# The first chunk's attention logits as one group of eighty matmuls, with the mask added by VectorE and the task order searched anew

## The chip, the cores and the metric

One core of a Trainium2 chip. The metric is the device time of one execution in microseconds; medians are given over several executions. Single core, so there is one span and one granted clock per run; an execution over 1.5% above the fastest of its kernel was classed as slow and left out of the ratios.

Short names: TensorE does the matmuls, VectorE the elementwise work on bf16 and the softmax sums, ScalarE the gelu, the exp and most copies out of PSUM ("evictions"), GpSimd the accumulating output writes, SyncE issues transfers. ScalarE also issues some transfers from its own instruction stream.

## The reference, cut to what matters

```python
def reference(A_x, A_wqkv, A_wo, B_x, B_w1, B_b1, B_w2, B_b2):   # x is 1 x 2048 x 640, bf16
    xn = _layernorm(x, axis=-1)
    return x + _A_ref(xn, A_wqkv, A_wo) + _B_ref(xn, B_w1, B_b1, B_w2, B_b2)
# _A_ref: 32 heads of 20; position s attends to s, s-2, s-4, ... s-14 (8 offsets, "w")
    mask = idx >= 0                                  # only the first 14 positions lose anything
    logits = jnp.einsum("bhsd,bhswd->bhsw", q, kg) * scale
    logits = jnp.where(mask[None, None, :, :], logits, -1e9)
    attn = _softmax(logits, axis=-1)
    o = jnp.einsum("bhsw,bhswd->bhsd", attn, vg)     # then @ wo
# _B_ref: gelu(xn @ w1 + b1) @ w2 + b2, with 1536 hidden units
```

The kernel handles the 2048 positions in four chunks of 512 ("chunk 0" to "chunk 3"). The mask concerns chunk 0 alone.

## The kernel before

It isn't written as loops. A small planner holds tasks with an engine, a guessed duration, a rank and their needs, runs them through a model of the engines, and emits them in the order in which the model started them. Each engine then executes its own list strictly in that order. A table of rank offsets, found by search, decides the order.

```python
RANK = {
    "ad02": 35.3, "av1": -101.7, "av2": 76.7, ...      # cut: 22 entries
}
...
        for wp in range(W // 2):                     # a pair of offsets; wp = 0..3
            ...                                      # qk{n}{wp}{i}: VectorE, q * shifted k -> "prod"
            if wp % 2:
                both = [("prod", "qk", n, wp - 1), pr]
                need = [...]
                pl.add(f"lg{n}{wp}", PE, 1.2, n - 1000, need, f("lg", n, wp), both + [L], slack=0.8)
        ...
        pl.add(f"m{n}", VE, 1.22, n - 1000, [f"lg{n}3"], f("max", n), [L, m])
        ...                                          # mx (subtract), ex (exp), ss (sum), ri (reciprocal), at (attn)
        pl.add(f"xs{n}", SE, 1.2, n - 1000, [f"at{n}"], f("xs", n), [at, ax])
        pl.add(f"xd{n}", DQ, 6.0, n - 1000, [f"at{n}"], f("xd", n), [at, ax])
        ...                                          # av: VectorE, v * broadcast attn -> "pv"; ad, ot: their sums -> oT
```

Logits are per-head sums of products, so TensorE makes them with a 0/1 matrix of heads: forty matmuls for four offsets. In chunk 0 each such group of forty ended in one more matmul, a row of ones times a row of mask values, which accumulates -1e9 into the masked places.

```python
    def do_lg(n, wp):
        L = get(("L", n), lambda: psL.tile([P, W, P], F32, tag="L", name="L"))
        for x in range(2):
            prod = tiles["qk", n, wp - 1 + x]
            logits(L, prod, wp - 1 + x)
        if n == 0:
            g = slice(2 * wp - 2, 2 * wp + 2)
            nc.tensor.matmul(L[0:H, g, 0:MW], lhsT=ones_r[:], rhs=maskrow[:, g, :],
                             start=False, stop=False, skip_group_check=True)
```

After the softmax the weights are broadcast over partitions by four transfers: two issued by SyncE, two by ScalarE.

The stream of matmuls uses four rotating PSUM banks (`psA`, tag "acc") for projections (`pps`) and the first MLP layer (`hps`). ScalarE empties them; when it is late, TensorE stands.

Task names: `pj` a projection group of five matmuls, `pc` its eviction, `pad` the copy of the last 14 columns of K or V into the next chunk's buffer, `lg` logits, `mk` the new mask instruction, `xb` the addition of the MLP's bias to x on VectorE, `xs` and `xd` the two halves of a broadcast, `av` the products with V. The first digit is the chunk.

Of the kernel before, what the change touches and what calls it, by code (L numbers as in the profile page):

```python
# [11 lines left out]
ALU = mybir.AluOpType  # L12
AX = mybir.AxisListType
BF16 = mybir.dt.bfloat16
F32 = mybir.dt.float32
PE, VE, SE, DQ = "pe", "ve", "se", "dq"


class Plan:
# [101 lines left out]
S, D, F, H, W, DIL = 2048, 640, 1536, 32, 8, 2  # L121
# [10 lines left out]
MASKED = -1e9  # L132
MW = 16
# [5 lines left out]


RANK = {
    "ad02": 35.3, "av1": -101.7, "av2": 76.7, "f10": 53.1, "f11": 23.2, "f12": 66, "f13": 190, "gj1": -337.3,
    "gj3": -98.6, "o01": -72.1, "o03": 12.1, "o22": 213.2, "pj11": -45.8, "pj30": 109.2, "pj32": 49.6, "qk1": 10.4,
    "qk2": 112.3, "rc1": -399, "st2": 79.8, "xb1": -67.6, "xb3": 55.5, "xn1": 47.4,
}


def make_plan(fns, offsets=RANK):

    pl = Plan(offsets)  # L150
# [6 lines left out]
    def f(kind, *a):  # L157
        return lambda: fns[kind](*a)

    def done(n, which):  # L160
        if n:
            return [f"pc{n}{which}{to}" for to in range(KT)]
        return [f"gc{bl}{g}" for bl in range(BPC) for g, parts in enumerate(GROUPS) if which in [p[0] for p in parts]]

    for n in range(NCH):
# [36 lines left out]
        for which, buf in enumerate((q, k, v)):  # L202
# [5 lines left out]
            if which:  # L208
                need = done(n - 1, which) if n else []
# [3 lines left out]
        L = ("L", n)  # L213
        for wp in range(W // 2):
            pr = ("prod", "qk", n, wp)
            for i in range(2):
                need = done(n, 0) + done(n, 1) + [f"pad{n}1"]
                pl.add(f"qk{n}{wp}{i}", VE, 1.42, base + 3.0 * wp + i, need, f("qk", n, wp, i), [q, k, pr])
            if wp % 2:
                both = [("prod", "qk", n, wp - 1), pr]  # L220
                need = [f"qk{n}{x}{i}" for x in (wp - 1, wp) for i in range(2)] + ([f"lg{n}{wp-2}"] if wp > 2 else [])
                pl.add(f"lg{n}{wp}", PE, 1.2, n - 1000, need, f("lg", n, wp), both + [L], slack=0.8)

        e, at, ax = ("e", n), ("attn", n), ("ax", n)
        m, rs, ss, z = ("m", n), ("rs", n), ("ss", n), ("prod", "z", n)
        pl.add(f"m{n}", VE, 1.22, n - 1000, [f"lg{n}3"], f("max", n), [L, m])
        pl.add(f"mx{n}", VE, 1.22, n - 1000, [f"m{n}"], f("sub", n), [L, m, z])
        pl.add(f"ex{n}", SE, 1.02, n - 1000, [f"mx{n}"], f("exp", n), [z, e], table="exp")
        pl.add(f"ss{n}", VE, 1.93, n - 1000, [f"ex{n}"], f("sum", n), [e, ss])
# [6 lines left out]
        for wp in range(W // 2):  # L236
            for i in range(2):
                need = [f"xd{n}", f"xs{n}", f"pad{n}2"] + done(n, 2)
                pl.add(f"av{n}{wp}{i}", VE, 1.42, base + 15.0 + 6.0 * wp + i, need, f("av", n, wp, i), [v, ax, prs[wp]])
        for k2, (a, b, r) in enumerate(((0, 1, 9.0), (2, 3, 21.0), (0, 2, 22.0))):  # L240
            need = [f"av{n}{x}{i}" for x in (a, b) for i in range(2)] if k2 < 2 else [f"ad{n}0", f"ad{n}1"]
# [8 lines left out]
        for bl in range(BPC):  # L250
# [4 lines left out]
            for pc in range(5):  # L255
                need = [last] if last else [f"ge{n}{ft}" for ft in range(FT)] + [f"xb{n}", "ld"]
# [15 lines left out]
def kernel(  # L272
# [16 lines left out]
    nc = tc.nc  # L289
# [6 lines left out]
    consts = ctx.enter_context(tc.tile_pool(name="consts", bufs=1))  # L296
# [46 lines left out]
    nc.gpsimd.memset(eps_t[:], EPS)  # L343
    warm = consts.tile([P, 1], F32, name="warm")
    nc.scalar.activation(warm[:], eps_t[:], ACT.Sqrt)
    ones_r = consts.tile([1, H], BF16, name="ones_r")
    nc.gpsimd.memset(ones_r[:], 1.0)
    maskrow = consts.tile([1, W, MW], BF16, name="maskrow")
    nc.gpsimd.memset(maskrow[:], 0.0)
    for w in range(1, W):  # L350
        nc.gpsimd.memset(maskrow[:, w, 0 : DIL * w], MASKED)
    head_of = consts.tile([P, H], BF16, name="head_of")
    b1T = consts.tile([P, FT], F32, name="b1T")

# [17 lines left out]
    tiles = {}  # L372

    def get(key, make):
        if key not in tiles:
            tiles[key] = make()
        return tiles[key]
# [139 lines left out]
            op=ALU.mult,  # L517
        )

    def do_lg(n, wp):  # L520
        L = get(("L", n), lambda: psL.tile([P, W, P], F32, tag="L", name="L"))
        for x in range(2):
            prod = tiles["qk", n, wp - 1 + x]
            logits(L, prod, wp - 1 + x)
        if n == 0:
            g = slice(2 * wp - 2, 2 * wp + 2)
            nc.tensor.matmul(
                L[0:H, g, 0:MW],
                lhsT=ones_r[:],
                rhs=maskrow[:, g, :],  # L530
                start=False,
                stop=False,
                skip_group_check=True,
            )

    def logits(L, prod, wp):
        for t in range(KT):
            for j in range(BPC):
                nc.tensor.matmul(
                    L[j * H : (j + 1) * H, 2 * wp : 2 * wp + 2, :],  # L540
                    lhsT=head_of[:],
                    rhs=prod[:, :, t, j * P : (j + 1) * P],
                    start=(t == 0 and wp % 2 == 0),
                    stop=(t == KT - 1 and wp % 2 == 1),
                    skip_group_check=True,
                )
# [155 lines left out]
    with tc.manual_schedule(engines=engines):  # L702

        idle = psA.tile([P, CH], F32, tag="acc", name="idle")
        for _ in range(WARM):
            nc.tensor.matmul(idle[:, 0:P], lhsT=ident[:], rhs=ident[:], start=True, stop=True)
        for t in make_plan(fns).run():
            t["fn"]()
# [30 lines left out]
```

## Time and profile before

| | |
|---|---|
| median, lowest, highest of the first 3 executions | 217.23, 216.60, 220.82 us |
| profiled span | 215.8 us |
| TensorE, VectorE, ScalarE busy | 208.0, 180.8, 107.2 us |
| TensorE idle, as drawn, 26 to 212 us | 0.7 us in three waits |
| chain of waits that ended last | TensorE 48%, VectorE 28%, transfers 16% |

Here is the stretch of that chain, for the kernel before (start, us, what):

```profile
52.90 1.57 SPq L596
54.52 6.85 DMA ax<-attn
...
82.71 1.49 DVE oT L627
84.20 1.40 DVE prod L513
...
97.70 0.59 ACTq L596
98.33 6.25 DMA ax<-attn
104.70 2.89 DVE pv L612 x2
...
115.46 7.02 DVE pv L612 x5
122.50 0.59 ACTq L596
123.13 1.68 ACTq L596
124.86 0.59 ACT vT L498
125.49 1.24 PE pps L463 x5
```

Read it from the bottom. It leads from a group of TensorE's matmuls at 125.49 through ScalarE's eviction of V, two transfer issues on ScalarE's own stream (ACTq) and VectorE back to the landing of the first broadcast at 61.4. The chain also crosses the second broadcast, 98.33 to 104.58, but over the same stretch VectorE works on five products of its own, to 104.68, and waits for that broadcast only 0.02 us.

### The profile page before, as it was taken

To read this page: it belongs to the slowest core of one execution; us is meant where nothing else is said; L and a number is where in the kernel's file an instruction comes from. 1 tells how busy PE (TensorE), PEld (TensorE's weight loads), DVE (VectorE), ACT (ScalarE), POOL (GpSimd) and SP (SyncE) were. 2 spreads that over 40 slices of the span, in tenths; PEclk is the share of its full clock that TensorE was granted. 3 is DMA by queue.
4 is the path that set the end of the run, shared out by engine and by line. 5 is a ranking of instruction groups with operands and counts; after the bars stand their busy time and mean duration, and the time that the engine had idled before them with its cause. 6 is when DMAs were issued, how large, how long until landed. Compare 5 with 4: busy or idle time off the path is not lost.

```text
span 215.8 us, 3941 instructions
## 1 busy us (share of the span) xinstructions
PE 208.0 (96%) x1669; PEld 121.6 (56%) x1692; DVE 180.8 (84%) x170; ACT 107.2 (50%) x190; POOL 14.5 (7%) x33
## 2 busy tenths in 40 slices
PE   7799999999999999999999999999999999999994
PEld 7699945555454545555555545566545455555552
DVE  3649899769989999999999999998999999982001
ACT  3466895796937476553276075213763521351210
POOL 2000000000000000101011000111100011101220
PEclk9999999999999999999999999999999999999999
DMA  6999316926981313507220370222111522215223
GB/s 219 364 365 355 76 30 160 390 74 153 254 82 30 61 30 33 152 0 156 74 30 0 38 186 3 30 33 27 20 18 19 176 30 27 20 17 122 33 30 62
DMA packets 21449, 21.49 MB, mean 100 GB/s; under 512 B 9016, under 2 KB 18616, under 8 KB 21432
## 3 DMA queue, kind: packets, MB, share of 16 engines
q1 hardware_dynamic: 17832, 16.49, 27.2%
q0 software_dynamic: 2160, 2.46, 9.6%
q10 hardware_dynamic: 1440, 2.29, 3.8%
q8 instruction: 13, 0.21, 0.4%
q14 instruction: 4, 0.03, 0.1%
HBM read 10.00 MB, written 5.08 MB: 70 GB/s over the span
## 4 chain that ended last, share of the span: by engine, by line
PE 48%; DVE 28%; DMA 16%; SPq 3%; issue 2%; ACTq 1%; ACT 1%; DVEq 0%
PE lo L665 18%; PE hps L634 14%; DVE pv L612 10%; PE gps L480 6%; DMA ax<-attn 6%; PE hi L667 6%; DMA wv_sb<-in_A_wqkv_dram 5%; DMA b2bc<-in_B_b_dram 5%; DVE pv L621 4%; DVE prod L513 3%; PE pps L463 3%; DVE ssum L574 3%; DVE x_sb L440 2%; DVE attn L586 2%; DVE rs L581 1%
## 5 line engine op out<-in xcount | busy, mean ns | idle before, releaser
L634 PE MATMUL hps<-xnT,w_sb 128*128 128x512 bf16 x236 | 54.2, 379 | 0.2
L665 PE MATMUL lo<-w_sb,hT 128*128 128x512 bf16 x183 | 51.9, 379 | 0.0
L612 DVE TENSOR_TENSOR pv<-vT,ax 128x2560 bf16<-128x2560 bf16 x32 | 45.8, 1485 | 0.6 <-DMA ax<-attn 0.5
L513 DVE TENSOR_TENSOR prod<-qT,kT 128x2560 bf16<-128x2560 bf16 x32 | 45.5, 1483 | 0.1
L667 PE MATMUL hi<-w_sb,hT 128*128 128x128 bf16 x192 | 40.3, 219 | 0.5
L645 ACT ACTIVATE hT<-hps,b1T 128x512 bf16<-128x512 f32 x48 | 31.7, 687 | 16.5 <-PE hps L634 14.6
L634 PEld LDWEIGHTS <-w_sb 128*128 128x128 bf16 x240 | 22.9, 98 | 26.5
L621 DVE TENSOR_TENSOR pv<-pv 128x5120 bf16<-128x5120 bf16 x12 | 33.8, 2824 | 0.3
L665 PEld LDWEIGHTS <-hT 128*128 128x128 bf16 x192 | 18.7, 98 | 22.7 <-issue 0.6
L672 ACT CAST osb<-lo 128x512 bf16<-128x512 f32 x15 | 8.8, 584 | 42.7 <-issue 22.8
L678 POOL DMA_DIRECT2D out_dram<-osb x15 | 13.1, 873 | 195.1 <-ACT osb L673 195.1
L665 PE MATMUL lo<-wo,oT 128*128 128x512 bf16 x77 | 22.6, 379 | 0.0
L667 PEld LDWEIGHTS <-hT 128*128 128x128 bf16 x192 | 18.4, 98 | 1.5
L463 PE MATMUL pps<-xnT,wv_sb 128*128 128x512 bf16 x72 | 17.2, 379 | 0.4 <-ACT vT L498 0.3
L667 PE MATMUL hi<-wo,oT 128*128 128x128 bf16 x80 | 16.9, 219 | 0.3 <-issue 0.2
L463 PE MATMUL pps<-xnT,wk_sb 128*128 128x512 bf16 x71 | 16.9, 380 | 0.3
L463 PE MATMUL pps<-xnT,wq_sb 128*128 128x512 bf16 x75 | 16.8, 379 | 0.2 <-ACT qT L498 0.2
L383 DVE BATCH_NORM_STATS2 stats<-x_sb 128x6 f32<-128x320 bf16 x16 | 7.4, 460 | 8.4 <-DMA x_sb<-in_A_x_dram 8.4
L686 DVE TENSOR_TENSOR osb<-lo,x_sb 128x512 bf16<-128x512 f32 x1 | 0.7, 692 | 16.1 <-PE lo L665 16.1
L498 ACT CAST vT<-pps 128x512 bf16<-128x512 f32 x15 | 8.2, 596 | 11.3 <-PE pps L463 11.3
L665 PEld LDWEIGHTS <-oT 128*128 128x128 bf16 x80 | 7.8, 98 | 9.9 <-DVE oT L627 0.6
L463 PEld LDWEIGHTS <-wq_sb 128*128 128x128 bf16 x75 | 8.8, 117 | 7.8 <-issue 0.5
(63 smaller groups left out, 213.1 us busy)
## 6 DMA issues: line engine op xcount, KB each, us to landing
w_sb<-in_B_w_dram SPq DMA_DIRECT2D x2, 1920.0 KB, 10.8
out_dram<-osb POOLq DMA_DIRECT2D x15, 160.0 KB, 3.4
ax<-attn ACTq DMA_DIRECT2D x8, 256.0 KB, 5.7
ax<-attn SPq DMA_DIRECT2D x8, 256.0 KB, 5.3
x_sb<-in_A_x_dram SPq DMA_DIRECT2D x3, 640.0 KB, 10.9
out_dram<-x_sb SPq DMA_DIRECT2D x3, 640.0 KB, 3.5
wq_sb<-in_A_wqkv_dram SPq DMA_DIRECT2D x1, 800.0 KB, 5.0
wk_sb<-in_A_wqkv_dram SPq DMA_DIRECT2D x1, 800.0 KB, 8.6
```

Of the source, the lines that this page charges most:

```text
L463: nc.tensor.matmul(ps[:], lhsT=wqkv_p[which][:, ti, to, :], rhs=xnT[:, ti, :], start=(ti == 0), stop=(ti == KT - 1),)
L480: nc.tensor.matmul(ps[:, i, :], lhsT=wqkv_p[which][:, ti, to, :], rhs=tiles["xnT", 0][:, ti, cs], start=(ti == 0), stop=(ti == KT - 1),)
L498: nc.scalar.copy(dest[:, to, off : off + CH], tiles["pps", n, which, to][:])
L513: nc.vector.tensor_tensor(out=prod[:, i, :, :], in0=qkv_tile(n, 0)[:], in1=qkv_tile(n, 1)[:, :, off : off + CH], op=ALU.mult,)
L612: nc.vector.tensor_tensor(out=pv[:, i, :, :].rearrange("p t (j c) -> p t j c", j=BPC), in0=qkv_tile(n, 2)[:, :, off : off + CH].rearrange( ...
L621: nc.vector.tensor_tensor(out=ta[:], in0=ta[:], in1=tb[:], op=ALU.add)
L634: nc.tensor.matmul(ps[:], lhsT=w1_sb[:, ti, ft * P : (ft + 1) * P], rhs=tiles["xnT", n][:, ti, :], start=(ti == 0), stop=(ti == KT - 1),)
L645: nc.scalar.activation(hT[:], tiles["hps", n, ft][:], ACT.Gelu_apprx_tanh, bias=b1T[:, ft : ft + 1], scale=1.0)
L665: nc.tensor.matmul(lo[:], lhsT=lhs, rhs=rhs[:, 0:CH], start=first, stop=last)
L667: nc.tensor.matmul(hi[:, 0 : D - CH], lhsT=lhs, rhs=rhs[:, CH:D], start=first, stop=last)
L672: nc.scalar.copy(osb[:, 0:CH], tiles["lo", n, bl][:])
L678: nc.gpsimd.dma_start(rows, tiles["osb", n, bl][:], accum_op=ALU.add)
```

## The change

Intent: two mask matmuls and one entry into a group of logit matmuls less for TensorE, in exchange for one small VectorE instruction. The rank table was searched anew for it, so the order of tasks changes on all engines as well.

```diff
 RANK = {
-    "ad02": 35.3, "av1": -101.7, "av2": 76.7, ... "xb1": -67.6, "xb3": 55.5, "xn1": 47.4,
+    "ad02": 77, "av2": -4.2, ... "rc3": -86.1, "st2": 49.8, "st3": 51.7, "xn2": 23.8,
 }                                                      # cut: 22 entries each
-            if wp % 2:
-                both = [("prod", "qk", n, wp - 1), pr]
-                ...
-                pl.add(f"lg{n}{wp}", PE, 1.2, n - 1000, need, f("lg", n, wp), both + [L], slack=0.8)
+            group = 2 if n else 4
+            if wp % group == group - 1:
+                wps = range(wp - group + 1, wp + 1)
+                ...
+                pl.add(f"lg{n}{wp}", PE, 0.16 + 0.52 * group, n - 1000, need, f("lg", n, wps), every + [L], slack=0.8)
...
+        if n == 0:
+            pl.add("mk", VE, 0.26, n - 1000, ["lg03"], f("mask"), [L])
...
-    maskrow = consts.tile([1, W, MW], BF16, name="maskrow")
+    mask = consts.tile([H, W, MW], F32, name="mask")
...
+    def do_mask():
+        L = tiles["L", 0]
+        nc.vector.tensor_tensor(out=L[0:H, :, 0:MW], in0=L[0:H, :, 0:MW], in1=mask[:], op=ALU.add)
```

## The prediction

> **What bounds the kernel now.** I read the page's busy line first, then its forty slices, the waits of TensorE, a table of busy time by stretch, and last TensorE and VectorE in order of time around the first chunk's logits.
>
> ```profile
> PE 208.0 (96%) x1669; PEld 121.6 (56%) x1692; DVE 180.8 (84%) x170; ACT 107.2 (50%) x190; POOL 14.5 (7%) x33
> ...
> PE   7799999999999999999999999999999999999994
> ...
> DVE  3649899769989999999999999998999999982001
> ```
>
> TensorE is busy in every slice from the third to the last but one; VectorE nearly so, but it has only its two last evictions left after the thirty-seventh. A busy TensorE row is no proof, so I asked what it waits for between 26 and 212 us:
>
> ```profile
> PE pps L463 <- ACT vT L498: 0.3, 1, 0.3
> PE pps L463 <- ACT qT L498: 0.2, 1, 0.2
> PE hi L667 <- issue: 0.2, 1, 0.2
> ```
>
> Three waits, 0.7 us in 186. The stretches say the same (after the stretch: its length, then busy us and count of PE, PEld, DVE, ACT, POOL, then clock, DMA share, GB/s):
>
> ```profile
> 26.50:60.00 33.50, 33.29 (x233) 17.33 (x239) 30.01 (x33) 26.74 (x43) 0.00 (x0) 1.00 0.62 174
> 60.00:110.00 50.00, 49.27 (x395) 27.05 (x393) 49.16 (x34) 24.18 (x41) 2.09 (x3) 1.00 0.34 65
> 110.00:160.00 50.00, 49.42 (x357) 26.71 (x361) 49.03 (x32) 24.73 (x41) 4.97 (x6) 1.00 0.25 41
> ```
>
> So the time is the start until all of wqkv is there (13.1 us), then one dense stream of matmuls to 212.8, then some 3 us of tail. The chain of waits goes through VectorE between 45 and 124 us; this doesn't make VectorE the bound, because TensorE leaves no gap there: two engines run side by side, both nearly full, and whichever is late at a meeting point stops the other. Only what shortens the TensorE stream, or makes it wait, moves the end. The part that changes, in order of time (start, us, engine, line):
>
> ```profile
> 26.50 6.64 PE L634 MATMUL hps<-xnT,w_sb 128*128 128x512 bf16 x29
> 33.07 1.28 PE L539 MATMUL L<-prod,head_of 128*32 128x256 bf16 x40
> 34.27 0.20 PE L527 MATMUL L<-maskrow,ones_r 1*32 1x64 bf16 x1
> 34.41 2.33 PE L634 MATMUL hps<-xnT,w_sb 128*128 128x512 bf16 x9
> 36.58 2.32 PE L463 MATMUL pps<-xnT,wk_sb 128*128 128x512 bf16 x10
> 38.83 1.28 PE L539 MATMUL L<-prod,head_of 128*32 128x256 bf16 x40
> 40.03 0.20 PE L527 MATMUL L<-maskrow,ones_r 1*32 1x64 bf16 x1
> 40.16 3.43 PE L463 MATMUL pps<-xnT,wk_sb 128*128 128x512 bf16 x14
> ...
> 59.71 1.28 PE L539 MATMUL L<-prod,head_of 128*32 128x256 bf16 x40
> 60.92 0.39 PE L665 MATMUL lo<-w_sb,hT 128*128 128x512 bf16 x1
> ```
>
> The reader should take starts, not durations, from it: forty logit matmuls plus mask hold the stream from 33.07 to 34.41; forty without a mask from 59.71 to 60.92. And VectorE's side:
>
> ```profile
> 40.27 1.22 DVE L552 TENSOR_REDUCE m<-L 128x128 f32<-128x1024 f32 x1 [1.08 <-PE L L527]
> 41.52 1.22 DVE L559 TENSOR_TENSOR z<-L,m 128x1024 f32<-128x1024 f32 x1
> ...
> 45.44 1.49 DVE L440 TENSOR_TENSOR x_sb<-x_sb,b2bc 128x2560 bf16<-128x2560 bf16 x1 [2.13 <-DMA b2bc<-in_B_b_dram]
> ```
>
> VectorE has holes right here, 1.08 and 2.13 us.
>
> **What the Trainium skill says.** "Perfetto Trace Analysis", § Identifying the Most-Contended Engine, warns that matmul busy share is no measure of headroom, because matmuls are pipelined. The trace agrees: each 128x512 matmul is drawn as 379 ns, yet 25 follow each other in 5.39 us on the chain, 216 ns each. "TensorE: Matmul & The Clock Gate", § Back-to-back issue gap, gives N/2.4 + 2.5 ns for a warm stream, 216 ns at N = 512: the same number. For N up to 64 it has a floor of about 25 ns; here the 64-column mask matmul costs the stream some 130 ns, so the page's figure doesn't cover it (it has its own weights, of one row). "VectorE: DVE Perf Modes", § Why PSUM operands drop a tier, says that fp32 from PSUM runs at one element per cycle; the last eviction, 128 fp32 elements from PSUM, took 0.29 us in the trace and is my measure for the mask instruction, of the same 128 elements. "PSUM — Partial Sum Buffer", § Terms, has TensorE and VectorE collide in the same bank and quadrant whatever the columns; so the new instruction must wait for all eighty matmuls. No run shows such a collision.
>
> **The change part by part.**
> - Mask matmuls: 34.41 − 33.07 = 1.34 and 40.16 − 38.83 = 1.33 with mask, 60.92 − 59.71 = 1.21 without: 0.13 us each, 0.26 us off the TensorE path.
> - Two groups of forty become one of eighty. Entering a group costs: the thirty first-layer matmuls from 26.50 should give way at 26.50 + 30 x 0.2157 = 32.97, and the logits start at 33.07: 0.10 us. Inside, single starts in the trace step by 0.109 us for every four, ten times four is 1.09, but the group holds 1.21: 0.12 us of fill at its ends. One group less saves 0.22 us.
> - Together 0.48 us of TensorE time. Everything else on TensorE is the same work in another order.
> - VectorE: one instruction more, about 0.29 us plus 0.03 of hand-over between dependent instructions, in a hole.
> - GpSimd's mask constant covers 32 partitions instead of one: as many elements per partition, off the path.
> - The rank table is new, so tasks move on all engines. By program order, seven first-layer groups and four K projections come before the eighty logits; the two early bias additions on VectorE move ahead of the sum; the last of chunk 0's input copies leave ScalarE some 1.8 us earlier (one activation before them instead of four), so the weights behind them, and b2bc, land earlier.
>
> Where does the first softmax land? TensorE: 26.50 + 11 groups x 1.08 = 38.4; eighty matmuls 0.10 + 2 x 1.09 + 0.12 = 2.4, done at 40.8. Mask to 41.2, max to 42.4, subtract to 43.7; before, subtract ended at 42.74: 0.9 us later. ScalarE has a copy, a normalisation (0.93) and a table load (1.28) to do after the pj1 group that follows the logits (evicted near 42.5), so exp ends near 46.8 against 45.5. But both bias additions are then done (44.0 to 46.9), so sum, reciprocal and attn (1.9 + 1.0 + 1.2) end near 51.1: as before (51.03). The broadcast landed 8.5 us after its issue on SyncE at 52.90, which had waited for a bias addition; now it can be issued at 51.1 and land at 59.6 instead of 61.4. VectorE comes out 0.5 us ahead once I count the product it then still owes.
>
> Meetings after that, by adding measured durations. The second chunk's last logits: TensorE 40.8 + 13 x 1.08 + 4 x 0.81 + 1.3 + 20 x 1.08 = 81.0; VectorE 59.6 + 8 x 1.41 + 2 x 2.8 + 3 x 1.41 = 80.7. The first oT: TensorE wants it at 81.0 + 1.3 + 2 x 1.08 = 84.5, VectorE has it at 80.7 + 2.8 + 1.4 = 84.9: a wait of 0.4 us. The third chunk's logits come out 0.3 us on the right side, later meetings over 1 us.
>
> Sum: 217.23 − 0.48 − 0.5 (the two ScalarE waits of before, whose places are reordered) + 0.4 = 216.65. I say 216.6.
>
> **Rivals.**
> - A wait takes the place of what is saved. One group of eighty puts off the first softmax, and the meetings above are closer than the error of my sums (about 1 us). For: before is tight too. Against: waits at meetings don't add up, since a late TensorE gives VectorE time. It would give 217.5 to 219.
> - VectorE becomes the bound: it has 0.3 us more, but 16 us of idle before its last evictions. Before, the last oT was done at 195.9 and TensorE first read it at 199.06, so it would have to come 3 us later. Unlikely; 218 or more.
> - ScalarE holds PSUM: exp with its table load now stands between two evictions of projections, and four banks are about 4.3 us of TensorE stream. By my sums the stream meets the freed bank within 0.1 us. It would cost up to 1 us: 217.5.
> - The new order removes more than I see. The ceiling is small: 0.48 plus the 0.7 us of waits, plus perhaps 1 us of small gaps: 215.
>
> **Range and chances.** 216.6, with 215.5 to 218.2 for 8 in 10: below, the ceiling of what a full engine can give back; above, a missed meeting of one to two us. Executions of before already spread from 216.6 to 220.82. A gain over 2% (4.3 us) is beyond the ceiling: 0.02. A loss over 2% needs several missed meetings: 0.04. Within 2%: 0.94.
>
> **What would show it.** Right: logits of chunk 0 holding TensorE for about 2.4 us once, no one-row matmul, the mask at 0.26 to 0.32 us on VectorE near 41 us, attn near 51, TensorE's waits after 26 us below 1.5 us in total. Wrong: a wait of TensorE on VectorE's products or oT of over 1 us near 81 to 103 us, or on ScalarE's evictions near 47 us; a different time to 13.1 us; or the mask instruction taking half a microsecond or more.

## More of the kernel before

The tile `ax` has a single buffer.

```python
    def expand(queue, n, blocks):
        ax = get(("ax", n), lambda: axp.tile([P, BPC, W, P], BF16, tag="ax", name="ax"))
        for j in blocks:
            queue.dma_start(ax[:, j, :, :], tiles["attn", n][j * H : (j + 1) * H, :, :]
                            .unsqueeze(1).to_broadcast([H, NQ, W, P]))

    def do_xd(n):
        expand(nc.sync, n, (0, 1))

    def do_xs(n):
        expand(nc.scalar, n, (2, 3))
```

## The result, and the profile after

| | before | after |
|---|---|---|
| median of 6 executions each | 217.64 us | 215.13 us |
| lowest to highest | 216.60 to 220.82 | 214.64 to 215.50 |
| ratio (95% interval) | | 0.9888 (0.9850 to 0.9926) |
| profiled span | 215.8 us | 212.9 us |

A ratio is the mean time of one kernel's fast executions over that of the other's in the same rounds, so it isn't quite the ratio of the medians. The result counts as the same within 2%, as predicted, but at 215.13 us it lies below the predicted range, which began at 215.5. The gain is 1.1%, about four times the predicted 0.6 us.

The page of the changed kernel, busy line and chain of waits:

```profile
span 212.9 us, 3938 instructions
...
PE 206.3 (97%) x1667; PEld 121.4 (57%) x1690; DVE 181.0 (85%) x171; ACT 106.9 (50%) x190; POOL 14.4 (7%) x32
...
PE 95%; DMA 1%; DVE 1%; issue 1%; ACT 0%
```

The same chain line for the kernel before:

```profile
PE 48%; DVE 28%; DMA 16%; SPq 3%; issue 2%; ACTq 1%; ACT 1%; DVEq 0%
```

VectorE's busy time has hardly moved (180.8 to 181.0), but the last chain no longer passes through it: 28% became 1%. The waits of TensorE between 26 and 212 us, after:

```profile
PE hi L662 <- issue: 0.3, 2, 0.2
PE pps L465 <- issue: 0.2, 1, 0.2
```

No wait for ScalarE's evictions is left. (The three "issue" entries are places where a matmul's record is missing from the trace: the starts on both sides are two matmuls apart. A second profile of the changed kernel has more records and shows no wait at all in this view.)

TensorE of the changed kernel in order of time, then VectorE:

```profile
25.12 7.72 PE L629 MATMUL hps<-xnT,w_sb 128*128 128x512 bf16 x34
32.68 4.48 PE L465 MATMUL pps<-xnT,wk_sb 128*128 128x512 bf16 x19
37.09 2.37 PE L534 MATMUL L<-prod,head_of 128*32 128x256 bf16 x80
39.39 1.27 PE L465 MATMUL pps<-xnT,wk_sb 128*128 128x512 bf16 x4
```

```profile
39.51 0.29 DVE L529 TENSOR_TENSOR L<-L,mask 32x128 f32<-32x128 f32 x1 [1.46 <-PE L L534]
39.83 1.22 DVE L547 TENSOR_REDUCE m<-L 128x128 f32<-128x1024 f32 x1
41.09 1.22 DVE L554 TENSOR_TENSOR z<-L,m 128x1024 f32<-128x1024 f32 x1
...
42.51 2.89 DVE L442 TENSOR_TENSOR x_sb<-x_sb,b2bc 128x2560 bf16<-128x2560 bf16 x2
45.58 1.92 DVE L569 TENSOR_REDUCE ssum<-e 128x128 f32<-128x1024 bf16 x1 [0.19 <-ACT e L564]
...
48.52 1.23 DVE L581 TENSOR_TENSOR attn<-e,rs 128x1024 bf16<-128x1024 bf16 x1
49.67 7.09 DVE L515 TENSOR_TENSOR prod<-qT,kT 128x2560 bf16<-128x2560 bf16 x5
56.76 5.70 DVE L607 TENSOR_TENSOR pv<-vT,ax 128x2560 bf16<-128x2560 bf16 x4
```

The eighty logits hold the stream from 37.09 to 39.39, with the entry 2.4 us in all; the mask instruction took 0.29 us in a hole of 1.46; both bias additions (x2 at 42.51) lie before the sum; and the products with V start at 56.76 without a hole, where before they started at 61.39, after six products (x5 here) and a wait of 0.55 us for the broadcast. All of the first stretch stands 1.4 us earlier on the clock than predicted, because the first-layer matmuls began at 25.12 and not at 26.50.

**A measure that leaves the start out.** I therefore split every profile. S is the start of the first first-layer matmul (26.50 in the profile before, 25.12 after). D is the time from there to the first matmul of the last output block, and holds nearly all of the work that the change touches. Inside D, I take the distance of successive matmul starts from the trace: 215.7 ns between two 128x512 matmuls that nothing holds up. Whatever is longer than the usual distance of its kind by more than 0.1 us, and isn't a missing record, I count as a stall. D minus the stalls is TensorE's own work. Each row is one profiled execution. All profiles, in us ("dose" is extra VectorE work, explained with the experiments):

| profile | order | logits of chunk 0 | S | D | stalls | D − stalls |
|---|---|---|---|---|---|---|
| before | old | 2 groups, mask on TensorE | 26.50 | 181.53 | 1.01 | 180.52 |
| e0, before again | old | same | 25.08 | 182.08 | 1.57 | 180.52 |
| after | new | 1 group, mask on VectorE | 25.12 | 180.20 | 0.19 | 180.01 |
| e9, after again | new | same | 27.55 | 180.20 | 0.18 | 180.02 |
| e3 | new | 1 group, mask on TensorE | 25.02 | 180.35 | 0.18 | 180.17 |
| e4 | new | 2 groups, mask on VectorE | 25.18 | 181.35 | 1.12 | 180.23 |
| e11 | new | 2 groups, mask on TensorE | 25.48 | 181.64 | 1.16 | 180.49 |
| e16 | new | same, one issue moved | 25.01 | 180.67 | 0.18 | 180.49 |
| e10, e17 | new, one issue moved | 1 group, mask on VectorE; e17 with dose | 25.09, 25.19 | 180.20, 180.20 | 0.18, 0.18 | 180.02, 180.01 |
| e15, e18 | new | 1 group, mask on VectorE, dose, half dose | 25.01, 25.45 | 181.19, 180.77 | 1.21, 0.75 | 179.98, 180.01 |
| e5 | old | 1 group, mask on VectorE | 25.70 | 181.91 | 1.81 | 180.11 |
| e6, e7, e8 | old, moved | 2 groups, mask on TensorE | 24.98, 26.13, 25.04 | 181.40, 181.89, 181.45 | 0.88, 1.44, 0.99 | 180.52, 180.46, 180.46 |
| e14 | old | 2 groups, mask on TensorE, dose | 25.14 | 182.87 | 2.37 | 180.51 |
| e12 | old, moved | 2 groups, mask on TensorE | 25.18 | 181.14 | 0.69 | 180.46 |
| e13 | old, moved | 1 group, mask on VectorE | 24.96 | 180.65 | 0.67 | 179.98 |

The last column depends on the words of the kernel alone, within 0.1 us, whatever the order: 180.5 with two groups and the mask on TensorE, 180.0 to 180.1 with the changed form, and the two halves of the change (e3, e4) lie between. Everything else is stalls. Part of this is so by construction, as a stall is whatever exceeds the usual distance; what the column adds is the worth of each half, and that no large loss is spread over distances too short to count.

**Where the 2.9 us between the two spans are.** S differs by 1.38, D by 1.33 (work 0.51, stalls 0.83), and 0.2 lies in the end. Against e0, whose start was as early as that of after, D differs by 1.88 (work 0.51, stalls 1.38).

**S is chance.** The chain of waits of the kernel before, its first 15 us, and a line of TensorE from the same time:

```profile
2.74 10.33 DMA wv_sb<-in_A_wqkv_dram
...
13.11 1.59 PE gps L480 x25
```

```profile
10.87 1.31 PE L480 MATMUL gps<-xnT,wk_sb 128*128 128x128 bf16 x20 [0.65 <-DMA wk_sb<-in_A_wqkv_dram]
```

The chain of the changed kernel has no weight transfer in it:

```profile
7.58 4.07 PE gps L482 x70
11.65 0.28 PE tp L426 x5
11.93 1.40 PE gps L482 x25
```

Each transfer ends with sixteen completions. In the profile before, fifteen of the second x transfer's came between 6.46 and 7.06 us and the sixteenth at 8.55, and the weight transfers behind it kept that lag (fifteen by 9.27 and the last at 10.83; by 11.54 and 13.06). In the profile after, the sixteen came between 6.61 and 6.94. The programs issue the same loads there, and both kinds of start occurred with both kernels: the kernel before again started at 25.08, the changed kernel again at 27.55, with the first weight transfer's last completion at 8.30 in place of 6.02. The mean of S is 25.41 in the nine profiles of the old order and 25.41 in the ten of the new, so the start explains the difference of the first two spans, not the gain.

### The profile page after: what moved, and what is told of

Its sections match the earlier page's. It is cut to its first block, busy times and chain, and to the rows that moved or that the text cites. A ratio compares the mean times of both kernels' runs of the same rounds, so it can differ in the third digit from the quotient of the medians.

```text
span 212.9 us, 3938 instructions
## 1 busy us (share of the span) xinstructions
PE 206.3 (97%) x1667; PEld 121.4 (57%) x1690; DVE 181.0 (85%) x171; ACT 106.9 (50%) x190; POOL 14.4 (7%) x32
## 4 chain that ended last, share of the span: by engine, by line
PE 95%; DMA 1%; DVE 1%; issue 1%; ACT 0%
PE lo L660 27%; PE hps L629 24%; PE pps L465 23%; PE gps L482 8%; PE hi L662 8%; PE L L534 4%; DMA x_sb<-in_A_x_dram 1%; PE tp L426 0%; DVE stats L385 0%; DVE stats L386 0%; ACT xnT L430 0%; DVE xn L412 0%; DVE mv L387 0%; DVE osb L690 0%; PE b_tp L366 0%
## 5 line engine op out<-in xcount | busy, mean ns | idle before, releaser
L673 POOL DMA_DIRECT2D out_dram<-osb x15 | 13.1, 875 | 192.4 <-ACT osb L668 192.4
L500 ACT CAST kT<-pps 128x512 bf16<-128x512 f32 x15 | 8.8, 584 | 8.2 <-PE pps L465 8.2
L465 PEld LDWEIGHTS <-wk_sb 128*128 128x128 bf16 x75 | 8.6, 118 | 7.4 <-issue 0.4
```

What stands on the lines that cost most here:

```text
L465: nc.tensor.matmul(ps[:], lhsT=wqkv_p[which][:, ti, to, :], rhs=xnT[:, ti, :], start=(ti == 0), stop=(ti == KT - 1),)
L500: nc.scalar.copy(dest[:, to, off : off + CH], tiles["pps", n, which, to][:])
L673: nc.gpsimd.dma_start(rows, tiles["osb", n, bl][:], accum_op=ALU.add)
```

## The experiments

Every kernel below gave a correct result. Times were taken beside the kernel before on the same chip; each batch has its own runs of before. S and D are as defined above; E is S + D.

### First batch: which part of the change

**e0: the kernel before again**, no edit.

> The kernel before once more, against itself: it shows the noise and gives a second profile of its start. I call S the start of the first first-layer matmul (26.50 us before, 25.12 us changed) and D the time from there to the start of the last block's first matmul (181.53 us before, 180.20 us changed). Theory 'chance': S was late in the first profile only because one of sixteen DMA engines happened to run 1.6 us behind; then the last of the sixteen completions of the second x transfer may well come within 0.3 us of the others this time and S be near 25.1. Theory 'kernel': something in the kernel before makes one engine late every time; then S is 26.3 to 26.7 again. Both: D 181.5 plus or minus 0.2, ratio 1.00 plus or minus 0.006.

Ratio 0.9966 (0.9927 to 1.0005), medians 216.66 and 217.28: no difference, as it must be. Its profile, though, has the early start and yet D is 0.55 longer than in the first profile: of a start 1.42 us earlier, 0.87 reached the end. What VectorE waits for came earlier by less: the bias vector landed at 44.38 in place of 45.42. TensorE's waits in this run:

```profile
PE pps L463 <- ACT vT L498: 0.4, 1, 0.4
PE pps L463 <- ACT qT L498: 0.3, 1, 0.3
```

and the wait for V in order of time:

```profile
120.83 3.40 PE L463 MATMUL pps<-xnT,wv_sb 128*128 128x512 bf16 x15
124.63 1.24 PE L463 MATMUL pps<-xnT,wv_sb 128*128 128x512 bf16 x5 [0.39 <-ACT vT L498]
```

Fifteen matmuls from 120.83 at 215.7 ns give way at 124.07; the next started at 124.63. The stall is 0.56 us, but drawn as 0.39, since a matmul is drawn 0.38 long and only 0.216 of that is its own. A short stall doesn't show at all: two stalls of 0.28 and 0.22 us in this run are missing from the waits.

**e3: the new order, mask back on TensorE.**

```diff
+        if n == 0:
+            for g in (slice(0, 4), slice(4, 8)):
+                nc.tensor.matmul(L[0:H, g, 0:MW], lhsT=ones_r[:], rhs=maskrow[:, g, :], ...)
     def do_mask():
-        nc.vector.tensor_tensor(out=L[0:H, :, 0:MW], in0=L[0:H, :, 0:MW], in1=mask[:], op=ALU.add)
+        pass
```

> The changed kernel in its own order, with the mask back on TensorE: two one-row matmuls after the eighty, no mask instruction on VectorE. Theory 'TensorE stream': D is longer than in the changed kernel by the two mask matmuls, 0.26 us (180.46), whatever VectorE saves; time 0.1% over the changed kernel, ratio to before about 0.990. Rival 'VectorE hand-over': the mask instruction delays the softmax and its removal gives back 0.3 us or more: D 180.2 or less. If the late DMA engine comes from the kernel's constants (a one-row mask in place of 32 rows, which shifts what lies behind it), S is 26.5 here; if it is chance or the order, S is near 25.1.

Ratio 0.9913 (0.9876 to 0.9949); D 180.35, 0.15 above the changed kernel. The two mask matmuls, now in a row, cost the stream 0.15 us together, not 0.26. So the move of the mask to VectorE is by itself worth 0.15 us, and VectorE has the time for it.

**e4: the new order, two groups of forty, mask on VectorE.**

```diff
-            group = 2 if n else 4
+            group = 2
# and the order of the changed kernel kept, with lg01 put in after f105
```

> The changed kernel in its own order but the first chunk's logits in two groups of forty again (the first after six first-layer groups, as before); the mask stays on VectorE. Theory 'TensorE stream': one more entry and exit, D longer by 0.22 us (180.42), ratio to before about 0.990. Rival 'the single group brings the gain by what it lets the scheduler do': as the order is kept, the same 0.2 us and no more; a rise of D by over 0.5 us would mean that the group itself frees something else.

Ratio 0.9930 (0.9891 to 0.9970). D came out at 181.35, about 0.9 above what was expected. The work is as it should be, 180.23: one group costs 0.21. The rest is a stall of 0.94 us at 125 us, at the place where the old order has one too. The new order isn't free of that meeting; it only clears it, and this execution missed it. The 0.2 us of work alone didn't do that. VectorE's last product of chunk 1 ended 1.13 us later after S than in the changed kernel; 0.33 of this was there when attn of chunk 1 was done, and 0.79 came from a longer wait for chunk 1's broadcast, 2.15 us in place of this one:

```profile
101.30 2.90 DVE L607 TENSOR_TENSOR pv<-vT,ax 128x2560 bf16<-128x2560 bf16 x2 [1.36 <-DMA ax<-attn]
```

VectorE stands at this place in all ten profiles of the new order, for 0.85 to 2.15 us; in the nine of the old it waits there for 0.5 us at most.

**e5: the old order with the new words.**

```diff
 # the changed kernel, emitted in the old order:
-... qk021 lg01 ge05 ... st23 pj112 m0 ...
+... qk021 ge05 ... st23 pj112 mk m0 ...
```

> The kernel before in its own order on every engine, with only the change in words: one group of eighty where the second group was, one VectorE mask instruction ahead of the maximum, no mask matmuls. Theory 'order': the two waits of TensorE on ScalarE's evictions (0.37 us near 76, 0.43 us near 125) and a third of 0.2 us stay, and only 0.48 us goes: D 181.05, ratio to before 0.997 if S is as before. Rival 'structure': the change itself removes those waits: D 180.2. If the constants set S, it is near 25.1 here; if the order or the old kernel's other parts do, 26.5.

Ratio 0.9989 (0.9943 to 1.0034): no gain. D was expected at 181.05 and measured at 181.91, a miss. The work fell by 0.4, to 180.11, and the stalls rose by 0.24 over e0, to 1.81. The same 0.4 us that the new order keeps is lost here: what TensorE saves it waits for. A fixed number says who it waits for. From the end of VectorE's last product of chunk 1 to E it is 85.56 us in before, 85.56 in e0 and 85.61 in e5, while S varies by 1.4. In the old order the end hangs on VectorE (and on what stands between: the two issues and the eviction).

### Second batch: which waits hold the old order

Theory after the first batch: VectorE paces the old order up to about 125 us and passes its lateness on through ScalarE's stream, at two places: ScalarE's two transfer issues for the third broadcast (chunk 2's), near 122 us, and a copy of V's padding near 75 us, which waits for a VectorE product because V has two buffers. Rival: these waits are incidental.

**e6: in the kernel before, ScalarE's half of the third broadcast issued by SyncE.**

```diff
     def do_xs(n):
-        expand(nc.scalar, n, (2, 3))
+        expand(nc.sync if n == 2 else nc.scalar, n, (2, 3))
```

> The kernel before with one thing moved: the half of the third chunk's broadcast that ScalarE issues is issued by SyncE. In three runs in the old order the stretch from the end of VectorE's 16th value product (av131) to the last block's first matmul was 85.56, 85.56 and 85.61 us, although the start differed by 1.4 us: theory 'meeting' says that ScalarE, held at this issue until VectorE frees the buffer (121.6 us) and then for 2.3 us by the issue, frees PSUM too late and TensorE stands 0.4 to 0.9 us near 124. Then here: no wait near 124, that stretch 0.4 to 0.6 us shorter (85.0 to 85.15), ratio to before 0.9975 plus or minus 0.001. Rival 'dense stream': the end follows the start and TensorE's own sum; the wait moves elsewhere and the ratio is 1.000.

Ratio 0.9957 (0.9926 to 0.9989). The stall at 124 us is gone, D is 181.40, and the distance from VectorE's last product fell to 84.84: that link was cut. The stalls at 74 to 76 us stayed (0.88 together).

**e7: in the kernel before, the padding copy later on ScalarE.**

```diff
-... pc200 ... pc201 pad22 pc202 ... pc203 pc204 pc210 ...
+... pc200 ... pc201 pc202 ... pc203 pc204 pad22 pc210 ...
```

> The kernel before with the third chunk's V padding copy put three Q evictions later on ScalarE, so that its wait for VectorE (to about 75.6 us) no longer stands ahead of an eviction. Both theories: TensorE's wait of 0.37 to 0.51 us near 75 is gone. Theory 'meeting': this gains nothing, as the meeting near 124 sets the end; the wait there grows by as much (to 0.8 to 1.1 us), the stretch from av131 to the last block stays 85.55 plus or minus 0.1, ratio to before 1.000. Rival 'waits add up': the end comes 0.4 us earlier, ratio 0.998.

Ratio 1.0000 (0.9978 to 1.0023). The stall at 75 us is gone, but one of 0.99 us took its place at 83 us, where the first oT, VectorE's attention output of chunk 0, is wanted, and the distance from VectorE's last product stayed at 85.57. The wait near 124, which was expected to grow to 0.8 to 1.1, was 0.33. Removing one wait only let TensorE run into the next.

**e8: both edits.**

> The kernel before with both moves: the issue on SyncE and the padding copy later. Theory 'meeting': now both waits are gone, D (first first-layer matmul to the last block's first matmul) is 0.9 to 1.1 us under that of the kernel before with an early start (182.08), so 181.0 to 181.2; ratio to before 0.995. Rival: the two add nothing together, ratio 0.998 or more.

Ratio 0.9988 (0.9968 to 1.0009), D 181.45 where 181.0 to 181.2 was expected: a miss. (e6, with a D within 0.05 of this, was timed at 0.9957: so much do timed ratios differ without a difference in the profiles.) This is TensorE at the first oT in e8:

```profile
83.14 0.39 PE L708 MATMUL lo<-wo,oT 128*128 128x512 bf16 x1 [0.71 <-DVE oT L670]
```

The stall is 0.87, nearly all that is left in the run. In e6 and in e8 it is 123.40 us from the end of the first oT to E: VectorE paces both, only through another door. Rescheduling ScalarE can't mend that; VectorE has to reach the first oT earlier.

**e9: the changed kernel again**, no edit.

> The changed kernel once more, on this chip. Ratio to before 0.989 plus or minus 0.003, D 180.2 plus or minus 0.2 unless a broadcast lands late. If its first profile was lucky in the start, S can now be 25.5 to 26.5 with the end later by as much, as its end follows TensorE's stream; if the changed kernel's start is always early, S is 25.0 to 25.2 again.

Ratio 0.9923 (0.9892 to 0.9955), medians 215.14 and 217.00. Its start was 2.4 us late (S = 27.55), and D is 180.20 to the hundredth. So where the new order meets no stall at 125, the end follows TensorE's start at a constant distance, while in the old order it follows VectorE's last product.

### Third batch: can the old order have what the new one has

One thing that the new order does to VectorE: the addition of the bias to chunk 1's x (`xb1`) needs the bias vector, which lands at 44.4 us in e0 and 45.4 in the first profile. In the old order VectorE waits for it with the softmax's sum behind it. In the new order the vector is there earlier (it lands at 41.0, and both additions begin at 42.51), and the addition for chunk 2 is put off to 160 us.

**e12: in the kernel before, xb1 after the second oT**, where VectorE is less pressed.

```diff
-... m0 mx0 rc2 rc3 xb1 ss0 ri0 at0 ... ad12 ot1 av200 ...     (VectorE's list)
+... m0 mx0 rc2 rc3 ss0 ri0 at0 ... ad12 ot1 xb1 av200 ...
```

> The kernel before in its own order but one VectorE instruction moved: the second chunk's bias addition, which stands ahead of the first softmax's sum and waits there for b2bc, comes after the second oT. The sum then follows the exp at once (44.1 instead of 45.8 us with an early start), and all of VectorE up to the meetings with TensorE comes 1.4 to 1.7 us earlier; TensorE's work and order are untouched. Theory 'VectorE sets the pace up to 125 us in the old order': TensorE's waits near 51, 75 and 124 go, D falls from 182.1 to 180.7 plus or minus 0.2, ratio to before 0.9945 plus or minus 0.002. Rival 'ScalarE's queue alone': its evictions stand behind the same instructions, so the waits stay: D 181.7 or more, ratio 0.999.

**e13: the same with the new group and mask.**

> As the run before, with the change in words besides: one group of eighty, the mask on VectorE. In the old order alone this change gained nothing (ratio 0.999), by theory because VectorE set the pace. With VectorE out of the way it should now be worth its 0.4 to 0.5 us on TensorE: D 180.2 to 180.4, 0.4 to 0.5 below the run before, ratio 0.992. Rival: the group of eighty is worth nothing in this order anyway (VectorE's later softmax eats it): D as in the run before.

Ratios 0.9952 (0.9913 to 0.9992) and 0.9915 (0.9874 to 0.9955). Both D came out above their expectations, 181.14 and 180.65, but the difference between them was as expected, 0.49. The stalls at 75 us are gone, none stands at 83, the one at 122 to 124 has shrunk to 0.22 in both, and the excess is one new wait, of 0.46 and 0.45 us, at the third oT. In e12's waits it stands as

```profile
PE lo L708 <- DVE oT L670: 0.3, 1, 0.3
```

Without it both would be at 180.68 and 180.20, which is what was expected; I hadn't foreseen that the 1.4 us of xb1, put after the second oT, would be missing at the third. Two things follow. One moved VectorE instruction brings the stalls of the old order from 1.57 (e0) to 0.69, a new one of 0.46 included, so they were VectorE's. And the words of the change are worth 0.49 us once VectorE is out of the way, against nothing in e5.

**e11: the new order alone**, two groups, masks on TensorE.

```diff
 # the kernel before, emitted in the order of the changed kernel; lg01 after f105, no mk
```

> The order of the changed kernel on every engine, with two groups of forty and both mask matmuls on TensorE as before, no VectorE mask: the reordering alone. Theory: the order removes the waits and TensorE's stream sets the end; D 180.6 to 180.7 (180.2 plus 0.22 for the second group and 0.15 to 0.26 for the masks), ratio 0.993. Rival 'the mask and the group bring it': D 181.5 or more. A late second broadcast may add up to 0.9 us near 124, as in the run with two groups.

Ratio 0.9921 (0.9883 to 0.9959): most of the gain, from the order alone. D in its profile is 181.64 against an expected 180.6 to 180.7, because of a stall of 0.97 us at 125.5, like e4's; the work is 180.49. The profiled execution, at 216.71 us, was the slowest of the six, whose median is 215.64. The product that VectorE must finish first is 97.7 us after S here and 97.9 in e4, but 96.8 and 97.0 in the two profiles of the changed kernel.

**e10: the changed kernel with e6's edit.**

> The changed kernel with ScalarE's half of the third chunk's broadcast issued by SyncE, so that a late VectorE can't hold up the evictions near 124 us. Theory: where the changed kernel has no wait there nothing is gained, D 180.2 plus or minus 0.1; runs in which a broadcast comes late gain up to 0.9 us, so the median may be 0.0 to 0.3 us better; ratio to before 0.990. Rival: the longer issue on one queue makes the third broadcast land later and TensorE waits for the second oT near 130: D 180.5 or more.

Ratio 0.9885 (0.9847 to 0.9924), D 180.20. The lowest median, 214.92 us, but not to be told from the changed kernel's.

### Last batches: how much room the new order has

Open were why e4 and e11 lose more than their work, and whether VectorE really paces the old order while TensorE is drawn busy. The test is a dose: the same extra 0.96 us for VectorE in both kernels.

```diff
     def do_recip(n):
-        nc.vector.reciprocal(rs[:], tiles["ss", n][:])
+        for _ in range(2 if n == 1 else 1):
+            nc.vector.reciprocal(rs[:], tiles["ss", n][:])
```

**e14: that in the kernel before.**

> The kernel before with the reciprocal of the second chunk's softmax done twice: 0.96 us more work for VectorE near 95 us, nothing else. Theory (VectorE sets the pace of the old order up to its last product of chunk 1, near 122 us, and the end follows 85.5 us behind that instruction): D, the time from the first first-layer matmul to the last block, rises from 181.5 to 182.1 by 0.8 to 1.0 us, to 182.4 to 183.1, and the distance from that VectorE instruction to the last block stays 85.5 to 85.7. Rival, what the prediction said (TensorE leaves no gap, so VectorE has room): D stays 181.5 to 182.1.

D 182.87, in the expected range; the distance from VectorE's last product 85.59, as in the four runs before it. Stalls 2.37, work 180.51. The ratio, 1.0010 (0.9975 to 1.0045), doesn't resolve 0.8 us in 217.

**e15: that in the changed kernel.**

> The changed kernel with the same doubled reciprocal. In its two profiles TensorE finds its next bank free about 0.5 to 0.9 us before it needs it near 125 us. Theory (the new order gave VectorE room, but less than one doubled reciprocal of it): D rises from 180.20 by 0 to 0.5 us, to 180.2 to 180.7, less than half of what the kernel before pays. Rival (the new order only moved the same coupling, VectorE sets the pace in it too): D rises by the full 0.96, to 181.1 to 181.2.

D 181.19: it rose by 0.99, the whole dose. My theory's number is missed and the rival's is met; what follows shows that this isn't the dose passed on. The stalls are 0.74 at 124.8 and 0.28 at 96.7. Ratio 0.9962 (0.9919 to 1.0004). ScalarE in e15:

```profile
122.80 2.32 ACTq L592 DMA_DIRECT2D ax<-attn  x2
125.16 1.07 ACT L500 CAST vT<-pps 128x512 bf16<-128x512 f32 x2 [3.53 <-issue]
```

and in the changed kernel:

```profile
121.95 1.47 ACTq L591 DMA_DIRECT2D ax<-attn  x2
123.47 1.07 ACT L500 CAST vT<-pps 128x512 bf16<-128x512 f32 x2 [1.98 <-PE pps L465]
```

The pair of issues began 0.85 later and took 0.85 longer, so the eviction that frees TensorE's bank came 1.7 later. The pair took 1.5 to 1.7 us in the three profiles (after, e3, e9) that lose nothing there, and 2.3 to 2.8 in all others that issue it from ScalarE.

The pair's length counts in full. From VectorE's last product to E it is 83.42 to 83.43 us in e4, e15 and e18, whose pairs took 2.31 to 2.32, and 83.93 in e11, whose pair took 2.82; in the old order it is 85.56 with a pair of 2.31 (before) and 85.61 with one of 2.37 (e5). From this I estimate that with the changed kernel's pair of 1.47 the least distance is 82.58. The changed kernel had 83.40, so it had 0.82 us of room. The rise of D in e15 is then 0.96 (VectorE later) + 0.85 (the pair longer) − 0.82 (the room), and that this comes near the dose is luck. By the same estimate a short pair would have kept the meeting at 125; no run shows it.

**e16: e11 with e6's edit.**

> The new order with the old two groups and their masks on TensorE, and ScalarE's half of the third chunk's broadcast issued by SyncE. With that half on ScalarE this kernel's D was 181.64, with one stall of 0.97 us at 125.5 us. Theory (that stall is ScalarE's queue standing behind VectorE's last product of chunk 1 and then behind its own transfer issue): D 180.6 to 180.8, which is the TensorE work of this form, 180.49, and the stall of 0.18 near 46 us. Rival (VectorE is late as such, and the wait moves to the next thing that it owes, the second oT): D 181.2 to 181.7.

D 180.67, as the theory had it: e11's stall at 125 us is gone. This pair of runs isn't clean, though: VectorE's last product of chunk 1 also came 0.60 us earlier after S (97.12 against 97.72), where e3 lost nothing with the issue on ScalarE. That ScalarE's stream was enough to make the stall is seen in e11 itself: its pair of issues held the eviction of V for 2.82 us. Ratio 0.9948 (0.9904 to 0.9992).

**e17: the changed kernel with the doubled reciprocal and e6's edit.**

> The changed kernel, the third chunk's broadcast all on SyncE, and the doubled reciprocal (0.96 us more for VectorE). The doubled reciprocal alone cost the changed kernel 0.99 us of D (181.19 against 180.20). Theory (what is lost there is ScalarE's queue, held by VectorE's last product of chunk 1 and by its own transfer issue; the matmuls themselves have room): D 180.2 to 180.35. Rival (VectorE itself is on the path in the new order too): D 181.0 to 181.2.

D 180.20: the dose that cost 0.99 us costs nothing once SyncE issues that broadcast. Here too luck helped, as the product came at 97.26 after S and not at 97.76 (VectorE waited 0.85 us for chunk 1's broadcast, against 1.44 in e15); but e18 below, with the product at 97.33 and the issue on ScalarE, lost 0.57. Ratio 0.9945 (0.9901 to 0.9989). SyncE and ScalarE in e17:

```profile
122.47 4.04 SPq L592 DMA_DIRECT2D ax<-attn  x4
```

```profile
122.53 1.07 ACT L500 CAST vT<-pps 128x512 bf16<-128x512 f32 x2 [0.98 <-DVE pv L608]
```

The eviction of V still waits for VectorE's product, since it overwrites a buffer that the product reads, but it then starts at once, 2.6 us earlier than in e15, while SyncE spends 4 us on the issues, where nothing stands behind them.

**e18: the changed kernel with half a reciprocal more.**

```diff
+        if n == 1:
+            nc.vector.reciprocal(rs[:, 0 : P // 2], tiles["ss", n][:, 0 : P // 2])
```

> The changed kernel with half of the reciprocal done again: about 0.5 us more for VectorE. Theory (the new order clears this meeting by more than 0.3 and less than 0.7 us of VectorE time: the runs of it that lost nothing have the last product of chunk 1 at 96.6 to 97.1 us after the first first-layer matmul, those that lost about 1 us at 97.7 to 97.9): between the two, D 180.2 to 180.9, and if ScalarE's two transfer issues take 2.3 us in place of 1.5, at the upper end. Rival (the loss is in proportion to the delay): D 180.65 to 180.75.

D 180.77: inside the theory's band, at its upper end, with the pair of issues at 2.32 us; the rival's band ends 0.01 to 0.02 below. So the band doesn't tell a step from a proportion. The pairs do: in the new order the pair took 1.5 to 1.7 us where it began by 97.15 after S (after, e9, e3), and 2.3 or more where it began at 97.37 or later (e18, e11, e15, e4). A delay of a fifth of a microsecond goes with 0.85 us of longer issuing. So half a microsecond more for VectorE ahead of chunk 1's broadcast cost this kernel 0.57 us; work after that broadcast's issue, where VectorE stands for 1.36 us, wasn't tested. Ratio 0.9960 (0.9909 to 1.0011).

## Why the prediction was right or wrong

The direction, the class and the work on TensorE were right; the waits were not, and they make up most of the gain.

- **TensorE's work, −0.48.** Right. D without stalls fell from 180.52 to 180.01. The parts: one group less 0.21 (e4 against after; predicted 0.22), the masks 0.15 to 0.26 depending on whether they stand together (e3) or apart.
- **The mask on VectorE, 0.29 us in a hole.** Right: 0.29 us, in a hole of 1.46. It waits for all eighty matmuls, as the maximum did before.
- **The first softmax.** Right relative to the start of the first-layer matmuls: attn was predicted to end 24.6 us after it and did (49.75 − 25.12). The additions of the bias fitted before the sum.
- **The start to 13.1 us, taken as fixed.** Wrong as a number for one execution: S ranged from 24.96 to 27.55 in nineteen profiles, with the same mean in both orders. It isn't a part of the change.
- **"This doesn't make VectorE the bound, because TensorE leaves no gap there."** This is the step that failed. TensorE left gaps of 1.0 to 1.6 us in all, drawn as 0.5 to 0.7, and behind them was VectorE: the distance from its last product of chunk 1 to the end stayed at 85.56 to 85.61 in before, e0, e5, e7 and e14, through different starts, less TensorE work and more VectorE work, and removing one wait let TensorE run into another (e7, e8). The chain line with 28% of VectorE had said so.
- **The waits, −0.5 + 0.4.** The two terms that were mis-sized. The waits removed come to 0.83 us against the first profile and 1.38 against e0, counted from starts; the new wait of 0.4 us for the first oT didn't come. It rested on a broadcast of 8.5 us after its issue, copied from before; in the new order issue and landing took 7.0 us at most (49.78 to 56.76), and the first oT was done 57.1 us after S in place of 58.4.
- **The rivals.** ScalarE holding PSUM behind the exp: it happened, 0.18 us at 45.7, near the 0.1 of the sums. VectorE becoming the bound: not in the changed kernel, but half a microsecond more for VectorE already costs 0.57 (e18), with the longer pair of issues.
- **The range.** The ceiling that the prediction gave for "the new order removes more than I see" was 215; the measured 215.13 lies inside it. The range was cut at 215.5 by belief in the drawn gaps.

Put together, D fell by 1.33 or 1.88 us in the profiles; the timed ratios of the changed kernel, 0.9888 and 0.9923, are 2.4 and 1.7 us. About 0.5 of that is the change in its words, the rest is the waits that its order took away. In the old order the words alone gave nothing (e5); in the new order the words also bring VectorE nearer to the wait at 125 us in time (attn of chunk 1 is done 0.33 us later in e4 and 0.63 in e11), so the two parts aren't simply additive.

What stays open: why the same pair of transfer issues takes 1.5 us in some profiles and 2.3 in others. "Perfetto Trace Analysis", § Per-instruction lifecycle, says that the profiled time of such an issue includes waiting for the descriptor generator that the two issuing engines share. The trace doesn't settle it: issued by SyncE alone, in e10, the four took 0.54, 0.62, 1.04 and 1.65 us, so long ones occur with no second engine issuing beside them. No run separates waiting from generating. Open too are what makes chunk 1's broadcast land late in some executions of the new order, and what remains between the timed gain and D: 2.4 us (interval 1.6 to 3.3) against 1.33 or 1.88.

## What to carry to other kernels

A matmul row without drawn gaps doesn't mean that TensorE sets the pace: measure from start to start, and look for a distance to the end that stays the same when something else moves; where the chain of waits names a second engine for a quarter of the time, slow that engine down by a known dose and see what the end does. A saving on an engine that isn't the pacer is paid back as waiting (0.4 us of work saved in e5, no gain), so look for the pacer's next meeting before adding savings up. A transfer issue is work on the stream of the engine that issues it: put behind a late producer and ahead of an eviction, it hands on the lateness and adds its own length, and an idle engine should issue it.

## What the Trainium skill lacked or had wrong

- "TensorE: Matmul & The Clock Gate", § Back-to-back issue gap: a floor of about 25 ns for up to 64 columns. It says that its figures for few columns leave out the weight loads, and this section has none with them for so small a matmul. The 64-column mask matmul with weights of its own cost the stream 0.13 us behind a group of forty, and two in a row cost 0.15 us (e3).
- "DMA: Bandwidth & Descriptors", § Issuing engines are not separate DMA queues: calls the issuing time usually small relative to the transfer. Here a pair of issues on ScalarE took 1.5 to 2.8 us, with transfers that landed 5.4 to 6.5 us after their issue, and D was 0.57 us shorter with it on SyncE (e17 against e18, VectorE's product within 0.07 us of the same place).
- The same page, § Latency and other measured facts, calls two of the sixteen DMA engines usually slower and ties this to transfers issued by GpSimd. Here loads issued by SyncE had one late completion of sixteen in some executions only, by 1.5 us in the first profile, and two in e9, the later one by 2.3; the loads behind them kept the lag (S was 26.50 and 27.55). The trace doesn't name the engine.
- "Perfetto Trace Analysis", § Identifying the Most-Contended Engine, warns against matmul busy time, but doesn't say by how much drawn gaps fall short: a stall of 0.56 us was drawn as 0.39, and stalls of 0.22 and 0.28 us weren't listed as waits at all (e0).
